# One written order for all five engines of an attention-and-Fourier kernel, with the MLP weights in four transfers

## The chip, the cores and the metric

The kernel runs on one core of one Trainium2 chip. A core has five engines that this kernel uses: TensorE (PE, matrix products, with a weight load that the profile lists as PEld), VectorE (DVE), ScalarE (ACT), GpSimd (POOL) and SyncE (SP, which here only issues transfers). The metric is the device time of one execution in microseconds, smaller is better; the figure of a kernel is the median of its runs.

## The reference, cut to what matters

Two stages follow each other. The first is block-sparse causal attention for 4 batches, 8 heads, 768 positions and head size 64: every query keeps its own block of 64 keys and the three blocks with the highest gate score. The second takes the heads side by side as a 768 x 512 matrix per batch, adds the real part of its two-dimensional Fourier transform, normalizes each row, and runs a two-layer MLP (512 to 2048 to 512) with a residual.

```python
k_rep = k.reshape(B, H, n_blocks, block, D).mean(axis=3)
gate_scores = np.einsum('bhsd,bhnd->bhsn', q, k_rep)      # causal blocks only
top_idx = np.argsort(gate_scores, axis=-1)[..., -top_k:]
scores = scale * np.matmul(q, k.transpose(0, 1, 3, 2))    # masked to those blocks, causal
attn = np.exp(scores - max); attn = attn / sum
x = np.matmul(attn, v)                                    # -> (B, 768, 512)
# ...
u = x + np.real(fft(fft(x, axis=1), axis=2))
un = (u - mean(u)) / np.sqrt(var(u) + 1e-06)
out = u + np.maximum(un @ w_ch1, 0.0) @ w_ch2
```

## The kernel before: the parts that the change touches

Heads are worked on in pairs, so there are 16 pairs P = 0 to 15, four to a batch. The steps of a pair and of a batch have short names, which the texts below use:

| name | what it does | engine |
|---|---|---|
| Lk, Lq, Lv | loads k, q, v of a pair | SyncE |
| tk, tq | six 128x128 transposes of k or q | PE |
| ks, kc, qc, qs | sums of k by block, copies of k and q | DVE, ACT, DVE, GpSimd |
| g, gt, gx, gm, K | gate scores, transpose, top three, mask, mask into the k/q rows | PE, DVE, DVE, DVE, GpSimd |
| s, e, d | one of six score tiles, its exponential, its causal edge | PE, ACT, GpSimd |
| vc, v, x | copy of v to 16 bits, product with v, division by the sums | GpSimd, PE, DVE |
| fs, fd, f (fa, fb) | folds of x over rows and columns, before the Fourier products | DVE |
| y, ty, tr, m, u, xu, xt, un | Fourier products, copies, second product, u, centred x, its transpose | PE, ACT, DVE, PE, DVE, ACT, PE, DVE |
| w, r | one of 16 tiles of the first MLP layer, its ReLU | PE, ACT or DVE |
| c, o | second MLP layer for 128 rows, residual | PE, DVE |

Attention for the first seven pairs and 12 of batch 0's MLP tiles stand in one written list, `HEAD`, in whose order all five engines work. What comes after is woven from two lists by weights, with only SyncE's order fixed; the other four engines' order is left to the scheduler of the tile framework.

```python
HEAD = """
Lkq:2 Lv:0 Lv:1 tk:0 tq:0 Lkq:3 tk:1 ks:0 qc:0 ks:1 g:0 gt:0 tq:1 Lkq:4 gx:0 tk:2 gm:0 qc:1 qs:0
# ... 16 lines cut
gm:5 d:4,2 kc:6 v:3 d:4,4 e:4,3 x:3 qs:6 s:5,2 s:4,5 s:5,5 e:5,2 fs:3 s:5,0 e:4,5 s:5,4 s:5,1 Lw:2
d:4,5 e:5,5 s:5,3 fd:3 e:5,0 g:6 fb:0 e:5,1 fa:0 d:5,5 e:5,4 Lw:3 d:5,2 gt:6 gx:6 vc:4 Lv:6 gm:6
d:4,3 y:1 y:0 d:4,1 v:4 d:5,0 ty:1 e:5,3 s:6,3 d:5,4 tr:1 ty:0 d:5,1 e:6,3 m:0 tr:0 s:6,4 x:4
# ... 6 lines cut
"""
# ...
    def fold_s(b, hp):                       # two DVE instructions in a row
        # ...
        tt(sd[:, 0, :, cols], x_b[:, 0:3, cols], x_b[:, 3:6, cols], ALU.add)
        tt(sd[:, 1, :, cols], x_b[:, 0:3, cols], x_b[:, 3:6, cols], ALU.subtract)
    # ...
    def fg_hi(b):                            # fg_lo is alike, for the other half
        fg, zw = fg_tile(b)
        tt(fg[:, :, 257:384], zw[:, :, 257:384], zw[:, :, 511:384:-1], ALU.subtract)
        tt(fg[:, :, 384:511], zw[:, :, 257:384], zw[:, :, 511:384:-1], ALU.add)
        nc.vector.tensor_copy(out=fg[:, :, 511:512], in_=zw[:, :, 384:385])
    # ...
    def load_w1(dt):                         # 4 of these, 128 rows x 2048 columns each
        nc.gpsimd.dma_start(out=w1_sb[:, dt, :], in_=moe_w_ch1[128 * dt:128 * (dt + 1), :])

    def load_w2(c):                          # 4 of these, 512 rows each
        nc.gpsimd.dma_start(out=w2_sb[:, 4 * c:4 * (c + 1), :],
                            in_=moe_w_ch2[512 * c:512 * (c + 1), :]
                            .rearrange("(it p) l -> p it l", p=128))
    # ...
    with tc.manual_schedule(engines={ET.SP, ET.PE, ET.DVE, ET.Activation, ET.Pool}):
        consts_first()
        for x in HEAD.split():
            n, a = x.split(":")
            HEAD_OPS[n](*[int(i) for i in a.split(",")])
    with tc.manual_schedule(engines={ET.SP}):
        for b in range(B):
            L = []
            for i in range(NP * (b + 1) + 1, min(NP * (b + 2) + 1, NPAIR + 1)):
                if i > 7:
                    L += attn_slot(i, i + 1, i + 2)
            weave(L, stream(b) if b else stream_0())
```

`tt` is `tensor_tensor` on DVE unless another engine is named. GpSimd's copies (`pcopy`, used by qs, K and vc) and the causal edges d are `affine_select` instructions with one input in the on-chip memory SBUF. The transfers that GpSimd issues turn the weights from 32 to 16 bits on the way.

Of the kernel before, what the change touches and what calls it, by code (L numbers as in the profile page):

```python
# [124 lines left out]
NW = 12  # L125


HEAD = """
Lkq:2 Lv:0 Lv:1 tk:0 tq:0 Lkq:3 tk:1 ks:0 qc:0 ks:1 g:0 gt:0 tq:1 Lkq:4 gx:0 tk:2 gm:0 qc:1 qs:0
kc:0 kc:1 s:0,2 kc:2 vc:0 Lv:2 qs:1 e:0,2 s:0,4 g:1 tq:2 Lkq:5 e:0,4 ks:2 d:0,2 gt:1 gx:1 s:0,5  # L130
qc:2 e:0,5 s:0,0 e:0,0 s:0,3 s:0,1 gm:1 g:2 s:1,2 e:0,1 s:1,3 gt:2 e:0,3 d:0,0 e:1,2 s:1,4 d:0,4
tk:3 gx:2 d:0,1 e:1,3 d:0,5 d:0,3 e:1,4 v:0 gm:2 qs:2 ks:3 x:0 s:1,0 kc:3 tq:3 Lkq:6 Lt:0 e:1,0
vc:1 Lv:3 s:2,0 s:1,1 s:1,5 qc:3 d:1,0 e:2,0 g:3 s:2,2 d:1,3 d:1,4 fs:0 e:1,5 gt:3 s:2,1 d:1,5
d:2,0 s:2,5 gx:3 e:1,1 tk:4 e:2,2 e:2,5 gm:3 d:1,2 d:1,1 s:2,3 e:2,1 tq:4 Lkq:7 v:1 ks:4 qs:3 qc:4
e:2,3 g:4 kc:4 d:2,1 x:1 gt:4 fs:1 s:2,4 gx:4 d:2,5 s:3,0 d:2,2 tk:5 e:2,4 s:3,2 qs:4 ks:5 e:3,0
vc:2 Lv:4 s:3,4 e:3,2 d:2,3 d:2,4 kc:5 v:2 s:3,3 Lc:0 gm:4 x:2 tq:5 Lkq:8 qc:5 fs:2 vc:3 Lv:5
e:3,4 s:3,5 s:4,1 e:3,3 s:3,1 s:4,0 fd:2 e:3,5 g:5 e:4,1 d:3,0 Lw:0 d:3,3 gt:5 gx:5 s:4,4 e:4,0
tq:6 e:3,1 qc:6 d:3,2 d:3,4 d:3,5 Lw:1 d:3,1 tk:6 Lkq:9 qs:5 e:4,4 s:4,2 d:4,0 e:4,2 ks:6 s:4,3
gm:5 d:4,2 kc:6 v:3 d:4,4 e:4,3 x:3 qs:6 s:5,2 s:4,5 s:5,5 e:5,2 fs:3 s:5,0 e:4,5 s:5,4 s:5,1 Lw:2
d:4,5 e:5,5 s:5,3 fd:3 e:5,0 g:6 fb:0 e:5,1 fa:0 d:5,5 e:5,4 Lw:3 d:5,2 gt:6 gx:6 vc:4 Lv:6 gm:6  # L140
d:4,3 y:1 y:0 d:4,1 v:4 d:5,0 ty:1 e:5,3 s:6,3 d:5,4 tr:1 ty:0 d:5,1 e:6,3 m:0 tr:0 s:6,4 x:4
s:6,0 e:6,4 u:0 m:1 u:1 d:5,3 e:6,0 m:2 u:2 xu:0 s:6,1 s:6,5 tq:7 qc:7 e:6,5 vc:5 Lv:7 xu:1 xt:0
tk:7 Lkq:10 e:6,1 un:0 ks:7 xt:1 d:6,5 xu:2 v:5 xt:2 un:1 un:2 kc:7 g:7 qs:7 s:6,2 Li:0 gt:7 w:10
gx:7 w:4 e:6,2 tk:8 x:5 r:10 r:4 w:11 gm:7 tq:8 Lkq:11 Lx:0 K:7 vc:6 Lv:8 kc:8 qc:8 w:0 d:6,0 ks:8
w:9 Lx:1 d:6,4 g:8 r:11 r:0 s:7,2 s:7,3 r:9 s:7,4 gt:8 d:6,1 d:6,3 d:6,2 gx:8 e:7,2 tq:9 e:7,4
qc:9 v:6 qs:8 e:7,3 fs:5 s:7,5 e:7,5 s:7,1 s:7,0 x:6 w:7 w:1 e:7,1 r:7 Lx:2 qs:9 w:5 e:7,0 r:5
fs:4 w:6 tk:9 Lkq:12 w:3 gm:8 fs:6 r:6 d:7,3 fd:6 ks:9 r:1 r:3 d:7,2 Lx:3 K:8 w:8 kc:9 w:2 d:7,5
r:8 d:7,0 r:2 d:7,1 d:7,4
# [5 lines left out]
def kernel(  # L154
# [58 lines left out]
    w1_sb = ctile([128, NDT, DF], F16, "w1_sb")  # L213
# [8 lines left out]
    dummy = ctile([128, 1], FP, "dummy")  # L222
    wsrc = bpool.tile([128, 512], F16, tag="hT0", name="zeros")
# [6 lines left out]
    hold = [None]  # L230

    def load(P, who, eng):
        if hold[0] is not None:
            hold[0].append((P, who, eng))
            return
        b, hp = divmod(P, NP)
        src = (q, k, v)[who]
        if who == 2:
            t = apool.tile([128, 2 * NST, 64], FP, tag="nat2", name=f"nat2_{P}", bufs=2)
            eng.dma_start(t, src[b, 2 * hp:2 * hp + 2].rearrange("e (st p) d -> p (e st) d", p=128))  # L240
            nat[P, 2] = t
            return
        if P >= NPAIR:
            return
        t = apool.tile([128, NST, 2, 64], FP, tag=f"nat{who}", name=f"nat{who}_{P}", bufs=3)
        for e in range(2):
            eng.dma_start(t[:, :, e, :],
                          src[b, 2 * hp + e].rearrange("(st p) d -> p st d", p=128))
        nat[P, who] = t
# [4 lines left out]

    def cast_v(P):
        v_cast(P)
        if P + 2 < NPAIR:
            load(P + 2, 2, nc.sync)
# [12 lines left out]
    def a_sums(P):  # L271
        ps = pairs[P]["tp", 1]
        kr12 = spool.tile([128, NB], FP, tag="kr12", name=f"kr12_{P}")
        nc.vector.tensor_reduce(out=kr12, in_=ps.rearrange("p (n c) -> p n c", c=64),  # L274
                                axis=mybir.AxisListType.X, op=ALU.add)
        tt((kr_s if P < NX else kr2_s)[P % NSLOT][:, :, 0:NB],
# [22 lines left out]

    def stage_A(P):  # L300
        a_tp(P, 1)
        a_sums(P)
        a_k(P)
        a_tp(P, 0)
        a_q32(P)
        a_q(P)
# [36 lines left out]
    def g_mask(P):  # L343
        d = pairs[P]
        mx = d["mx"]
        if P < NX:
            gt, l = d["gt"].rearrange("p (b n) -> p b n", n=32), lt[:, :, 0:NB]
            tt(l, gt[:, :, 0:NB], mx[:, :, 2:3].to_broadcast([128, 10, NB]), ALU.is_lt)
            tt(l, l, oth, ALU.mult)
            full = lt.rearrange("p b n -> p (b n)")  # L350
        else:
            full = apool.tile([128, 192], F16, tag="ltb", name=f"lt_{P}", bufs=1)
            tt(full.rearrange("p (j n) -> p j n", n=16),
               d["gt"].rearrange("p (j n) -> p j n", n=16),
               mx[:, :, 2:3].to_broadcast([128, 12, 16]), ALU.is_lt)
            tt(full, full, oth2, ALU.mult)
        mt = apool.tile([128, 320 if P < NX else 192], F16, tag="mt", name=f"mt_{P}", bufs=4)
        nc.vector.transpose(out=mt, in_=full)  # L358
        d["mt"] = mt

    def stage_G(P):
        g_mm(P)
        g_turn(P)
        g_max(P)
        g_mask(P)
# [48 lines left out]
    def stage_S(P, i):  # L414
        s_mm(P, i)
        s_exp(P, i)
        s_sel(P, i)

# [24 lines left out]
    def stage_V(P, e):  # L443
        v_mm(P, e)
        if e == 1:
            v_x(P)

# [3 lines left out]
    def fold_s(b, hp):  # L451
# [6 lines left out]
        tt(sd[:, 0, :, cols], x_b[:, 0:3, cols], x_b[:, 3:6, cols], ALU.add)  # L458
        tt(sd[:, 1, :, cols], x_b[:, 0:3, cols], x_b[:, 3:6, cols], ALU.subtract)

    def fold_d(b, hp):
        sd, zw = fold[b]
        cols = slice(128 * hp, 128 * hp + 128)
        if hp >= 2:
            sf = sd.rearrange("p a t d -> p (a t) d")
            lo = slice(128 * (hp - 2), 128 * (hp - 1))
            tt(zw[:, :, lo], sf[:, :, lo], sf[:, :, cols], ALU.add)
            tt(zw[:, :, cols], sf[:, :, lo], sf[:, :, cols], ALU.subtract)

    def stage_fold(b, hp):  # L470
        fold_s(b, hp)
        fold_d(b, hp)
# [8 lines left out]
    def fg_lo(b):  # L481
        fg, zw = fg_tile(b)
        tt(fg[:, :, 1:128], zw[:, :, 1:128], zw[:, :, 255:128:-1], ALU.add)
        nc.vector.tensor_copy(out=fg[:, :, 0:512:256], in_=zw[:, :, 0:512:256])
        nc.vector.memset(fg[:, :, 128:129], 0.0)
        tt(fg[:, :, 129:256], zw[:, :, 1:128], zw[:, :, 255:128:-1], ALU.subtract)

    def fg_hi(b):
        fg, zw = fg_tile(b)
        tt(fg[:, :, 257:384], zw[:, :, 257:384], zw[:, :, 511:384:-1], ALU.subtract)  # L490
        tt(fg[:, :, 384:511], zw[:, :, 257:384], zw[:, :, 511:384:-1], ALU.add)
        nc.vector.tensor_copy(out=fg[:, :, 511:512], in_=zw[:, :, 384:385])

    def stage_fg(b):
        fg_lo(b)
        fg_hi(b)

    ys, y_ps, m_ps, t_ps = {}, {}, {}, {}
# [33 lines left out]

    def stage_Y(b, h):
        y_mm(b, h)
        y_copy(b, h)
        y_turn(b, h)
# [39 lines left out]
    def stage_M(b, kp):  # L576
        m_mm(b, kp)
        m_u(b, kp)
        m_x(b, kp)
        if b not in (0, B - 1):  # L580
            stage_T(b, kp)

# [7 lines left out]
    def t_copy(b, kp):  # L590
        ps, dst = t_ps[b, kp], un_t[b][:, :, 256 * kp:256 * kp + 256]
        if b == 0 or kp < 2:
            nc.vector.tensor_copy(out=dst, in_=ps)
        else:
            nc.vector.tensor_copy(out=dst[:, :, 0:128], in_=ps[:, :, 0:128])
            nc.scalar.copy(out=dst[:, :, 128:256], in_=ps[:, :, 128:256])

    def stage_T(b, kp):
        x_b = x_t[b]
        if b in (0, B - 1):  # L600
            t_mm(b, kp)
            t_copy(b, kp)
            return
        for kt in range(2 * kp, 2 * kp + 2):
            nc.sync.dma_start_transpose(un_t[b][:, :, 128 * kt:128 * kt + 128], x_b[:, kt, :])

    def stage_R(b):

        mv, rs, _ = st_t[b]
        for kt in range(NST):  # L610
            bst = spool.tile([128, 6], FP, tag="bst", name=f"bst{kt}_{b}", bufs=4)
            nc.vector.bn_stats(out=bst, in_=u_t[b, kt // 2][:, kt % 2, :])
            nc.vector.bn_aggr(out=mv[:, kt, :], in_=bst)
        vr, t2 = [spool.tile([128, NST], FP, tag=n, name=f"{n}_{b}") for n in ("vr", "t2")]
        yi = rs.bitcast(I32)
        po = nc.gpsimd
# [5 lines left out]
                                op0=ALU.mult, op1=ALU.add)  # L622
        for _ in range(3):
# [6 lines left out]
    def w1_mm(b, it):  # L630
        unT = un_t[b]
        h_t[b, it, "p"] = hp = pst([128, S], f"h{it}_{b}")
        for dt in range(NDT):
            w1s = w1_sb[:, dt, 128 * it:128 * (it + 1)]
# [14 lines left out]
    def stage_W1(b, it):  # L649
        w1_mm(b, it)  # L650
        w1_relu(b, it)

    def stage_W2(b, sts, part):
        n = len(sts)
        if part == 0:
            h_t[b, "c"] = pst([128, n, 512], f"c{sts[0]}_{b}")
        cps = h_t[b, "c"]
        st = sts[part]
        for it in range(NIT):
            nc.tensor.matmul(cps[:, part, :], h_t[b, it][:, 128 * st:128 * (st + 1)],  # L660
# [153 lines left out]
    def run(L):  # L814
        for f, _ in L:
            f()
# [63 lines left out]
```

## Time and profile before

| | |
|---|---|
| time, median of 3 runs | 321.04 us (320.4 to 322.42) |
| span of the profiled execution | 321.2 us |
| mean granted TensorE clock | 0.983 |
| busy: DVE, ACT, POOL | 200.6 us, 166.7 us, 109.4 us |
| first transpose on PE, first instruction of W2 (`L660`) | 6.3 us, 107.7 us |
| last product of W2 ends, span ends | 317.4 us, 321.2 us |
| SyncE's loads and stores; GpSimd's weight transfers | 27.69 MB, 38.7% of 16 transfer engines; 4.19 MB as written, 8.0% |

In the profile's lines of groups, a line begins with the line of the kernel (L12), the engine and the operation; `fg<-zw` means that tile fg is written from tile zw; shapes are partitions x elements. Durations there are in nanoseconds, all other times in microseconds. A digit in the strip of 40 slices is the busy share of that slice (8 us each) in tenths. The granted clock is given as a share of full speed.

### The profile page before, as it was taken

Reading aid. Unit: us, or ns where it says so; the run is one execution under the profiler, and the core shown is the slowest. Engines: PE = TensorE matmul, PEld = TensorE weight load, DVE = VectorE, ACT = ScalarE, POOL = GpSimd, SP = SyncE. Lnnn points to the kernel's source line nnn. Section 1 sums busy time; section 2 is a strip of 40 time slices with the busy share of each in tenths; the row PEclk is TensorE's granted clock in tenths of the full one; section 3 lists DMA queues with packets and bytes.
Section 4 is the critical chain, followed back from the end, with each engine's and each line's share of the span. In section 5 each row is a group of like instructions: output and inputs, shape, how many; then the busy total and the mean of one; then the engine's idle time right before and its main releaser. Section 6 shows DMA issues by size and latency. Waiting matters only on the chain.

```text
span 321.2 us, 6693 instructions
## 1 busy us (share of the span) xinstructions
PE 298.7 (93%) x2638; PEld 180.4 (56%) x2638; DVE 200.6 (62%) x577; ACT 166.7 (52%) x206; POOL 109.4 (34%) x247
## 2 busy tenths in 40 slices
PE   8788976969998999989999999999999999999995
PEld 3456654656654545645666646645665565565442
DVE  2899999797794358975545549984314379421211
ACT  1688973775728444655767443637573124344000
POOL 2166295144894223346452524234220000200000
PEclk9999997999997999999999999999999999999999
DMA  9999999989993421169600012144000101100023
GB/s 175 217 214 217 259 198 220 228 168 168 202 155 70 98 74 43 35 139 253 152 0 2 0 56 61 35 131 117 0 2 0 43 24 68 65 2 0 0 82 116
DMA packets 88843, 32.83 MB, mean 102 GB/s; under 512 B 82592, under 2 KB 84972, under 8 KB 88812
## 3 DMA queue, kind: packets, MB, share of 16 engines
q1 hardware_dynamic: 83932, 27.69, 38.7%
q0 software_dynamic: 2688, 4.19, 8.0%
q10 hardware_dynamic: 2192, 0.52, 0.9%
q8 instruction: 21, 0.34, 0.4%
q14 instruction: 10, 0.08, 0.1%
HBM read 28.73 MB, written 6.29 MB: 109 GB/s over the span
## 4 chain that ended last, share of the span: by engine, by line
PE 66%; DVE 22%; ACT 7%; DMA 2%; issue 1%; SPq 1%; POOL 0%; DVEq 0%
PE c L660 22%; PE h L635 16%; PE h L637 8%; PE sc L390 6%; PE tp L269 4%; PE av L428 3%; ACT pt L405 3%; DVE sd L192 2%; DVE fg L192 2%; PE yp L508 2%; DVE kr L274 2%; DVE zw L192 2%; DMA nat<-in_k_dram 2%; DVE u L666 2%; DVE u L561 2%; DVE lt L192 1%
## 5 line engine op out<-in xcount | busy, mean ns | idle before, releaser
L405 ACT ACTIVATE pt<-sc 128x1024 f16<-128x1024 f32 (+1 forms) x96 | 84.0, 922 | 48.6 <-PE sc L390 41.6
L660 PE MATMUL c<-w_sb,hT 128*128 128x512 f16 x384 | 87.3, 379 | 0.0
L635 PE MATMUL h<-unT,w_sb 128*128 128x512 f16 x256 | 86.4, 383 | 0.6 <-ACT pt L405 0.6
L637 PE MATMUL h<-unT,w_sb 128*128 128x256 f16 x256 | 70.3, 275 | 0.0
L411 POOL TENSOR_SCALAR_AFFINE_SELECT pt<-pt 128x256 f16<-128x256 f16 x96 | 39.4, 426 | 82.2 <-ACT pt L405 81.7
L660 PEld LDWEIGHTS <-hT 128*128 128x128 f16 x384 | 36.8, 98 | 41.0 <-issue 0.5
L647 ACT ACTIVATE hT<-h 128x768 f16<-128x768 f32 x48 | 38.7, 810 | 31.1 <-PE h L637 30.8
L666 DVE SCALAR_TENSOR_TENSOR u<-c,rs,u 128x512 f32<-128x512 f32 x24 | 17.1, 742 | 40.1 <-PE c L660 40.1
L635 PEld LDWEIGHTS <-w_sb 128*128 128x128 f16 x256 | 25.1, 98 | 28.7 <-issue 1.7
L645 DVE TENSOR_SCALAR hT<-h 128x768 f16<-128x768 f32 x16 | 15.3, 955 | 34.6 <-PE h L637 34.5
L390 PE MATMUL sc<-qk 96*128 96x512 f16 (+3 forms) x144 | 27.8, 308 | 4.1 <-DVE hT L645 1.8
L269 PE MATMUL tp<-id,nat 128*128 128x128 f32 x192 | 26.1, 276 | 5.2 <-DMA nat<-in_k_dram 1.4
L637 PEld LDWEIGHTS <-w_sb 128*128 128x128 f16 x256 | 25.2, 98 | 4.9 <-issue 0.8
L195 POOL TENSOR_SCALAR_AFFINE_SELECT qk<-q 64x768 f16<-64x768 f32 (+1 forms) x25 | 20.6, 826 | 19.6 <-DVE q L290 18.9
L428 PEld LDWEIGHTS <-pt 128*128 128x128 f16 x672 | 23.7, 97 | 5.6 <-POOL pt L411 1.8
L269 PEld LDWEIGHTS tp<-id,nat 128*128 128x128 f32 x192 | 21.2, 141 | 10.0 <-issue 1.7
L428 PE MATMUL av<-v,pt 128*128 128x65 f16 x672 | 25.1, 193 | 1.2 <-POOL pt L411 1.2
L195 POOL TENSOR_SCALAR_AFFINE_SELECT v<-nat 128x768 f16<-128x768 f32 x16 | 14.8, 931 | 23.5 <-DMA nat<-in_v_dram 23.2
L195 POOL TENSOR_SCALAR_AFFINE_SELECT qk<-mt 32x384 f16<-32x384 f16 x36 | 18.7, 521 | 7.8 <-DVE mt L358 6.0
L573 ACT ACTIVATE x<-u,nm 128x512 f16<-128x512 f32 x24 | 15.8, 713 | 9.4 <-DVE nm L567 9.4
L390 PEld LDWEIGHTS <-qk 96*128 96x128 f16 x144 | 12.5, 99 | 13.8 <-issue 3.1
L285 ACT CAST qk<-tp 64x768 f16<-64x768 f32 x18 | 14.3, 793 | 10.4 <-DVE kr L274 10.3
(84 smaller groups left out, 352.8 us busy)
## 6 DMA issues: line engine op xcount, KB each, us to landing
nat<-in_v_dram SPq DMA_DIRECT2D x16, 384.0 KB, 5.7
nat<-in_k_dram SPq DMA_DIRECT2D x31, 192.0 KB, 5.3
nat<-in_q_dram SPq DMA_DIRECT2D x31, 192.0 KB, 4.0
out_dram<-u SPq DMA_DIRECT2D x11, 512.0 KB, 2.9
w_sb<-in_moe_w_ch_dram POOLq DMA_DIRECT2D x8, 512.0 KB, 7.9
fs_sb<-c_FS SPq DMA_DIRECT2D x1, 582.0 KB, 5.0
out_dram<-u SPq DMA_DIRECT2D x2, 256.0 KB, 2.0
fd_sb<-c_FD SPq DMA_DIRECT2D x1, 384.0 KB
```

The lines of the kernel that those rows point to most:

```text
L192: (eng or nc.vector).tensor_tensor(out=out, in0=in0, in1=in1, op=op)
L195: nc.gpsimd.affine_select(out=out, in_=in_, pattern=[[0, i] for i in n], base=0, channel_multiplier=0, compare_op=ALU.is_ge, fill=0.0)
L269: nc.tensor.transpose(ps[:, 128 * st:128 * st + 128], src[:, st, :], id32)
L390: nc.tensor.matmul(ps[:, e, co:co + q1 - q0], qk[0:96, e, 1, 128 * jt:128 * jt + 128], qk[0:96, e, 0, q0:q1], start=True, stop=True)
L405: nc.scalar.activation(out=d["pt"][:, o:o + 2 * n].rearrange("p (e c) -> p e c", e=2), in_=d["sc", i][:, :, 0:n], func=AF.Exp, scale=0.125)
L411: nc.gpsimd.affine_select(out=dg, in_=dg, pattern=[[0, 2], [1, 128]], base=0, channel_multiplier=-1, compare_op=ALU.is_ge, fill=0.0)
L428: nc.tensor.matmul(av[:, e, 66 * st:66 * st + 65], pt[:, co:co + 128], vv[:, e, jt, 0:65], start=(cnt == 0), stop=(cnt == 20))
L635: nc.tensor.matmul(hp[:, 0:512], w1s, unT[:, dt, 0:512], start=(dt == 0), stop=(dt == NDT - 1))
L637: nc.tensor.matmul(hp[:, 512:768], w1s, unT[:, dt, 512:768], start=(dt == 0), stop=(dt == NDT - 1))
L647: nc.scalar.activation(out=hT, in_=hp, func=AF.Relu)
L660: nc.tensor.matmul(cps[:, part, :], h_t[b, it][:, 128 * st:128 * (st + 1)], w2_sb[:, it, :], start=(it == 0), stop=(it == NIT - 1))
L666: nc.vector.scalar_tensor_tensor(out=o[:, i, :], in0=cps[:, i, :], scalar=st_t[b][1][:, sts[i]:sts[i] + 1], in1=o[:, i, :], op0=ALU.mult, ...
```

## The change

The written list now covers the whole kernel and is called `ORDER`; weaving, weights and held-back loads are gone, and all five engines follow the list to the end. Several steps are split so that the list can place their parts apart: `ks` becomes ks and kh, the mask becomes gl (two parts) and gm, each fold becomes two or four single instructions (fs, fd, f with a part number), the row statistics become bn for each 128 rows, nv and nr, a second-layer product becomes two halves of eight products (c:b,st,h), and each 128 rows of the output have their own residual (o) and store (od). Loads of k and q are placed one by one.

`pg` is new: GpSimd copies four elements, one from each of the four folded pieces f, so that it waits until all four are there. `w1_sb` becomes two tiles by column halves, and the weights come in four transfers (W:0, W:1, X:0, X:1) instead of eight.

The purpose is to have one order that is laid out as a whole, with GpSimd held back while DVE makes the folded pieces, and with the transfers of the weights put between GpSimd's copies.

```diff
-HEAD = """
-Lkq:2 Lv:0 Lv:1 tk:0 tq:0 Lkq:3 tk:1 ks:0 qc:0 ks:1 g:0 gt:0 tq:1 Lkq:4 gx:0 tk:2 gm:0 qc:1 qs:0
 (cut)
+ORDER = """
+Lq:1 Lk:1 Lq:2 Lk:2 tk:0 tq:0 ks:0 Lq:3 Lk:3 qc:0 tq:1 iz:1 kh:0 qs:0 g:0 Lq:4 Lv:0 Lv:1 qc:1 iz:0
 (cut)
+fd:3,1 s:4,2 gt:6 e:5,2 s:5,4 f:0,3 s:5,3 e:4,2 f:0,2 tk:8 f:0,1 e:5,4 y:0,1 f:0,0 e:5,3 ks:8
+d:5,4 d:4,2 y:0,0 tr:0,1 d:5,3 kc:8 W:0 gx:6 d:4,1 s:4,5 d:5,1 ty:0,1 tr:0,0 tk:7 d:5,0 pg:0 d:4,3
+e:4,5 ks:7 ty:0,0 m:0,2 W:1 gl:6,0 kc:7 d:5,2 m:0,1 u:0,2 d:5,5 vc:5 m:0,0 u:0,1 xu:0,2 d:4,4 Lv:7
+Lk:10 v:5 qs:6 u:0,0 qs:7 xu:0,1 xt:0,2 tq:8 xu:0,0 un:0,2 d:4,5 xt:0,1 kh:8 qc:8 xt:0,0 kh:7
+gl:6,1 v:4 qs:8 un:0,1 un:0,0 gm:6 g:7 vc:6 x:5 w:0,1 Lv:8 Lq:11 gt:7 x:4 w:0,3 r:0,1 gx:7 s:6,5
 (cut)
+e:10,5 K:11 Lv:14 Lq:15 xu:1,1 x:8 s:10,2 c:0,0,0 e:10,2 un:1,1 fs:8,1 d:10,4 fs:8,0 s:10,3 d:10,2
 (cut)
+c:3,1,1 o:3,4 od:3,4 c:3,5,1 o:3,1 od:3,1 o:3,0 od:3,0 o:3,5 od:3,5
 """
-    w1_sb = ctile([128, NDT, DF], F16, "w1_sb")
+    w1_s = [ctile([128, NDT, DF // 2], F16, f"w1_{c}") for c in range(2)]
+    gone = ctile([1, 4], F16, "gone")
 (cut)
-    def fg_hi(b):
-        fg, zw = fg_tile(b)
-        tt(fg[:, :, 257:384], zw[:, :, 257:384], zw[:, :, 511:384:-1], ALU.subtract)
-        tt(fg[:, :, 384:511], zw[:, :, 257:384], zw[:, :, 511:384:-1], ALU.add)
-        nc.vector.tensor_copy(out=fg[:, :, 511:512], in_=zw[:, :, 384:385])
+    def fg(b, i):
 (cut: i == 0 and i == 1)
+        elif i == 2:
+            tt(fg[:, :, 257:384], zw[:, :, 257:384], zw[:, :, 511:384:-1], ALU.subtract)
+            nc.vector.tensor_copy(out=fg[:, :, 256:257], in_=zw[:, :, 256:257])
+        else:
+            tt(fg[:, :, 384:511], zw[:, :, 257:384], zw[:, :, 511:384:-1], ALU.add)
+            nc.vector.tensor_copy(out=fg[:, :, 511:512], in_=zw[:, :, 384:385])
+
+    def fg_wait(b):
+        nc.gpsimd.tensor_copy(out=gone, in_=fg_tile(b)[0][0:1, 0, 127:512:128])
 (cut)
-    def load_w1(dt):
-        nc.gpsimd.dma_start(out=w1_sb[:, dt, :], in_=moe_w_ch1[128 * dt:128 * (dt + 1), :])
+    def load_w1(c):
+        h = slice(DF // 2 * c, DF // 2 * (c + 1))
+        nc.gpsimd.dma_start(out=w1_s[c],
+                            in_=moe_w_ch1[:, h].rearrange("(dt p) l -> p dt l", p=128))
     def load_w2(c):
-        nc.gpsimd.dma_start(out=w2_sb[:, 4 * c:4 * (c + 1), :],
-                            in_=moe_w_ch2[512 * c:512 * (c + 1), :]
+        nc.gpsimd.dma_start(out=w2_sb[:, 8 * c:8 * (c + 1), :],
+                            in_=moe_w_ch2[1024 * c:1024 * (c + 1), :]
                             .rearrange("(it p) l -> p it l", p=128))
 (cut)
-    with tc.manual_schedule(engines={ET.SP}):
-        for b in range(B):
-            L = []
-            for i in range(NP * (b + 1) + 1, min(NP * (b + 2) + 1, NPAIR + 1)):
-                if i > 7:
-                    L += attn_slot(i, i + 1, i + 2)
-            weave(L, stream(b) if b else stream_0())
+        for x in ORDER.split():
+            n, a = x.split(":")
+            WORK[n](*[int(i) for i in a.split(",")])
```

## The prediction

> **What bounds the kernel now.** I read the page first: the span, the busy shares and the strip of slices.
>
> ```profile
> span 321.2 us, 6693 instructions
> PE 298.7 (93%) x2638; PEld 180.4 (56%) x2638; DVE 200.6 (62%) x577; ACT 166.7 (52%) x206; POOL 109.4 (34%) x247
> ...
> PE   8788976969998999989999999999999999999995
> ...
> DVE  2899999797794358975545549984314379421211
> ...
> PEclk9999997999997999999999999999999999999999
> DMA  9999999989993421169600012144000101100023
> ```
>
> TensorE is busy 93% of the span, so a new order can win little more than its 22.5 us of idle time, its slow-clock time and the gaps inside "busy". All of that lies to the left: there PE's digits are 6 to 9, DVE's mostly 7 to 9, the transfer engines' 8 or 9. From slice 18 on PE is full. The windows put numbers on it (the columns are the stretch, its length, then PE, weight loads, DVE, ACT and POOL busy with counts, the granted clock, the transfer share and GB/s):
>
> ```profile
> 0.00:100.00 100.00, 85.88 (x1008) 56.32 (x1009) 84.27 (x253) 66.67 (x83) 52.60 (x117) 0.96 1.05 200
> 100.00:140.00 40.00, 37.38 (x305) 22.25 (x304) 27.26 (x82) 21.60 (x28) 13.68 (x25) 0.98 0.27 60
> 140.00:322.00 182.00, 175.47 (x1329) 101.87 (x1327) 89.10 (x245) 78.43 (x97) 43.08 (x105) 1.00 0.21 57
> ```
>
> PE idles 14.1 us in the first 100 us (and until the first transpose at 6.3 us it runs only warm-up products), 2.6 in the next 40, and 6.5 in the rest, of which 3.8 are the tail (the last product ends at 317.4). DVE is at 84% in the first stretch. What it does there is partly waiting inside instructions; the timeline of DVE, GpSimd and PE around the first fold:
>
> ```profile
> 49.12 4.20 DVE L192 TENSOR_TENSOR fg<-zw 128x762 f16<-128x762 f16 x2
> ...
> 49.30 0.55 POOL L728 DMA_DIRECT2D w_sb<-in_moe_w_ch_dram  x1
> 49.86 0.42 POOL L411 TENSOR_SCALAR_AFFINE_SELECT pt<-pt 128x256 f16<-128x256 f16 x1
> 50.22 0.91 POOL L195 TENSOR_SCALAR_AFFINE_SELECT v<-nat 128x768 f16<-128x768 f32 x1
> 51.07 1.83 POOL L411 TENSOR_SCALAR_AFFINE_SELECT pt<-pt 128x256 f16<-128x256 f16 x5
> ...
> 54.02 3.25 PE L508 MATMUL yp<-fs_sb,fg 128*128 128x193 f16 x19 [2.69 <-DVE fg L484]
> ```
>
> Two fg instructions take 4.20 us together; they end when GpSimd's unbroken row of work ends (52.9), and PE, which waited 2.69 us for fg, then makes 19 products in 3.25 us. The group of fg shows that this is no normal duration:
>
> ```profile
> L192 DVE TENSOR_TENSOR fg<-zw x16: 545/554/3635, 49.1 to 259.6; 128x762 f16<-128x762 f16 x16
> ```
>
> Median 554 ns, longest 3635 ns.
>
> **What the Trainium skill says.** "SBUF — State Buffer", section "Who interferes with whom": a DVE instruction with two SBUF inputs and a GpSimd instruction that reads SBUF contend for one port, and the one that comes second blocks for the other's whole duration. The trace agrees (554 against 3635 ns). "TensorE: Matmul & The Clock Gate", Part 1: an idle window of about 3.4 us halves the TensorE clock, and a busy one restores it. The trace agrees in kind: granted clock 0.83 between 40 and 60 us, around that wait, and yp products of 368 ns against a least of 243. "DMA: Bandwidth & Descriptors", section "Queues, rings and completion order": each transfer engine takes turns between the queues that have work. So GpSimd's weights and SyncE's loads should slow each other; here a weight transfer of 512 KB as written landed 7.2 to 8.7 us after issue, against 25.7/8 = 3.2 us of engine time (8.0% of the span over eight transfers).
>
> **The change, part by part.** The products stay the same. I price each step by its measured group: tk/tq 0.66 us, g 0.74 (early) or 0.46, a large score tile about 0.45, v 1.29, y 1.0 (1.5 with the extra row), m 0.87, a W1 tile w 1.30, half a W2 row block c 1.73. Over all steps PE comes to 277 us. As a test: the last 42.0 us of dense work (275.4 to 317.4) are priced at 16 x 1.30 + 12 x 1.73 = 41.6, so I add 1%: 280.
>
> *Contention, head.* Removed: the excess of the two-input DVE forms. fg is 16 x 752 ns mean against 545 least, 3.3 us; sd 32 x (484 - 345), 4.4 us; zw 16 x (634 - 546), 1.4 us; the copy in fg 0.7 us; masks and key sums some 3 us. Sum about 13 us of DVE time, nearly all before 100 us. `pg` is not in front of the folds but behind them; it is the placing that helps: in the list no GpSimd copy stands between f:0,3 and f:0,0, and d:5,4, GpSimd's next, waits for an exponential of that moment. I count 8 of the 13 us as gone. PE gains only what it waited for: the 2.7 us at the fold, and about 2 us of half clock after it.
>
> *Split steps.* Adds 4 small copies on DVE (about 0.18 us each) and, for the last batch, one whole copy on DVE in place of a half each on DVE and ACT: under 1 us, beside PE work.
>
> *Head as a whole.* I sum each engine's work in the list up to marks. Up to the first W2 half (c:0,0,0) DVE has 107.5 us: key sums and q copies 26.9, gate 28.2, x 9 x 1.18 = 10.6, folds 16.1, tr, u, un, bn, ReLU and the rest 25.5. PE has 92.8 there (W1 20.8, scores 23.8, transposes 17.1, v 12.9, g 7.5, y, m, xt 10.7). DVE starts its sums at 7.15 us, so if the list is laid out in time, as I read it, the first c cannot start before 7.15 + 107.5 = 114.7. It is *later* than now (107.7), with much more PE work in front. Now DVE idles 13.5 us between 7.15 and 107.7 (87.1 busy of 100.6: the first window's 84.3 less 0.9 before 7.15, and 3.7 after 100), and contention is extra. For the new list I allow 5 us for idle time and remaining contention together: first c at 119.5.
>
> *Rest.* Behind that mark PE has c 83.0, W1 62.4, scores 13.1, v 7.7, m 6.1, y 5.0, transposes 4.0, g 1.8, xt 1.3: 184.5, with 1% 186.4. DVE has 102 there, ACT 81, GpSimd 46, so PE bounds it. Stalls: 1.5 us, near the 1.9 us that PE idles between 140 and 317.4 now. The last residual (0.74 us) and store keep the tail at 3.8 us; the last store was already 256 KB.
>
> Sum: 119.5 + 186.4 + 1.5 + 3.8 = 311.2. I predict 311.
>
> **Rivals.** *The transfers become the bound.* A pair's k, q or v is 393 KB; at the 216 GB/s of the early slices that is 1.82 us, and all 48 take 87; the weights 25.7, tables and constants 5: 118 us. Summed in the list's order from 2.5 us on, the tables have landed at 49.0 where DVE's sum reaches their first use (y:0,1) at 49.3; W:0 at 64.5 against its use at 65.3; v of pair 3 at 38.9 against 38.8. There is no slack: the list is cut to the transfers as closely as to DVE. For: share 1.05 in the first 100 us; W:0 is twice as long as each old one and issued later, just after the first y, and shares turns with loads. Against: before landed all four quarters of W1 between 41.4 and 58. If transfers run 5% slower, the head slips 3 to 6 us: 314 to 317.
>
> *A fixed order stalls where the scheduler's did not.* An engine that meets an unready step stops though later ones are ready. For: the old written head is where PE idles; the stretch 140 to 240, woven, has PE at 98.75 of 100 us. Against: that head suffered from contention, and behind 120 us the list keeps W1 and W2 work between the attention steps. If each of the three later batch changes costs 3 us: 320, no gain.
>
> *Contention gone altogether and DVE full.* First c at 116, then no stall: 116 + 186.4 + 3.8 = 306. For: the marks of DVE, transfers and use agree within a microsecond, so the list was made with good durations. Against: nothing in the list keeps fs and fd clear of GpSimd.
>
> **Range and chances.** The 306 and the 317 are equally near; 305 to 318 holds both. Faster by over 2% means below 314.6, that is 3.6 us above my sum, well inside the first rival. I give it 0.72, within 2% 0.23, slower 0.05, since a loss of 6 us would need stalls where PE is now full.
>
> **What would show it.** Right: fg's longest duration under 1.5 us and the first y at 50 to 52 us (now 54.0); first W1 at 66 to 69 (now 73.1); first c at 117 to 122; DVE above 90% up to there; PE idle below 3 us between 140 us and the end of W2. The loads are the bound if PE or GpSimd wait longest for nat or w1 tiles. Wrong: PE idle of several us behind 120, or first c beyond 124.

## The result, and the profile after

| | before | after |
|---|---|---|
| time, median | 321.73 us (320.4 to 324.4, 4 runs) | 306.88 us (306.41 to 307.28, 4 runs) |
| span of the profiled execution | 321.2 us | 305.2 us |
| mean granted TensorE clock | 0.983 | 1.000 |
| PE idle in the span | 22.5 us | 13.4 us |
| first y, first w, first c | 54.0, 73.1, 107.7 us | 52.0, 66.0, 115.0 us |

The changed kernel takes 0.9528 of the time (95% interval 0.9461 to 0.9594): 14.9 us less. The page of the changed kernel:

```profile
span 305.2 us, 6705 instructions
...
PE 291.8 (96%) x2638; PEld 179.2 (59%) x2638; DVE 194.4 (64%) x581; ACT 163.2 (53%) x205; POOL 106.5 (35%) x247
...
PE   7789996999999999999999999999999999999994
...
PEclk9999999999999999999999999999999999999999
DMA  9999989999999998610110001112200011100013
```

PE makes the same 2638 products in 6.9 us less busy time; the clock strip, which had two slices below 9, has none. The transfers are now full to slice 16 (before: to slice 11): they were spread out over a longer head. The windows, in the columns used for the kernel before:

```profile
0.00:100.00 100.00, 90.91 (x1117) 61.37 (x1118) 85.17 (x290) 73.95 (x92) 52.91 (x111) 1.00 1.08 205
100.00:140.00 40.00, 39.87 (x387) 25.80 (x386) 34.28 (x106) 29.58 (x38) 27.08 (x59) 1.00 0.70 140
140.00:306.00 166.00, 161.04 (x1137) 92.08 (x1134) 74.95 (x188) 59.70 (x77) 26.48 (x78) 1.00 0.12 41
```

PE idles 9.1 us in the first 100 us instead of 14.1, 0.1 in the next 40 instead of 2.6. A third of the gain is not idle time at all: three stretches at half clock, shown below, took 5.1 us of PE's work in the kernel before, and now there are none. (A clock of 0.983 over 321.2 us makes 5.5 us; the rest of it lies behind the last product and costs nothing.) 9.1 us less idle time and 5.1 us of clock make 14.2 of the 16.0 us by which the span is shorter; the other 1.8 us are shorter busy time at full clock. The timeline of DVE, GpSimd and PE around the first fold of the changed kernel:

```profile
48.75 0.51 DVE L239 TENSOR_TENSOR fg<-zw 128x762 f16<-128x762 f16 x1
49.26 0.55 DVE L239 TENSOR_TENSOR fg<-zw 128x762 f16<-128x762 f16 x1
49.80 1.02 DVE L239 TENSOR_TENSOR fg<-zw 128x762 f16<-128x762 f16 x2
...
50.49 1.30 POOL L442 TENSOR_SCALAR_AFFINE_SELECT pt<-pt 128x256 f16<-128x256 f16 x3 [2.98 <-ACT pt L436]
51.74 0.96 POOL L713 DMA_DIRECT2D w<-in_moe_w_ch_dram  x1
...
52.01 1.78 PE L523 MATMUL yp<-fs_sb,fg 128*128 128x193 f16 x19 [2.04 <-DVE kr L311]
```

The four fg instructions take their 0.5 us each; GpSimd stood idle for 2.98 us just then. PE still waits 2.04 us, but the 19 products behind take 1.78 us, not 3.25. The wait is put down to DVE's kr, but when the same kernel was run again the products started at 50.7 us while kr ended at 51.8, so they do not need kr. They also wait for the Fourier table, whose load was issued only at 45.70, and in four of the later runs the wait in this place is named as the table's (`DMA fs_sb<-c_FS`; 0.6 us in three of them, 3.0 in the one with W1 earlier).

Where did the clock go? Windows of 2 us of the kernel before (length, PE busy, granted clock, transfer share, GB/s):

```profile
44.00:46.00 2.00, 1.23 (x26) 1.00 1.03 184
46.00:48.00 2.00, 1.32 (x20) 0.79 0.96 157
48.00:50.00 2.00, 2.00 (x24) 0.50 1.04 208
50.00:52.00 2.00, 1.34 (x20) 0.86 1.10 242
52.00:54.00 2.00, 0.00 (x0) 0.99 1.08 216
54.00:56.00 2.00, 1.98 (x13) 0.50 1.09 217
56.00:58.00 2.00, 2.00 (x15) 0.66 1.03 220
...
96.00:98.00 2.00, 0.43 (x2) 1.00 1.27 255
98.00:100.00 2.00, 2.00 (x17) 0.58 0.44 77
100.00:102.00 2.00, 2.00 (x10) 0.56 0.00 0
102.00:104.00 2.00, 2.00 (x17) 1.00 0.00 0
```

There are three stretches at half clock, each behind a thin stretch of PE. Their length follows from the columns: 54 to 58 us is 2 x (2.00 x 0.50 + 2.00 x 0.34) = 3.4 us, and the other two give 3.4 as well. Each takes 1.7 us of PE's work on top of the gap.

This is one execution, and not every execution of the kernel before has three such stretches. Over the 53 that ran beside the last group of experiments the mean clock lies between 0.983 and 0.995, 0.987 on average, which is a loss of 4 us and not of 5.5. The same 53 show what a stretch costs: the 20 at 0.983 or 0.984 have a median of 324.2 us, the 24 at 0.987 to 0.989 one of 322.6, the nine at 0.992 to 0.995 one of 321.0, so 1.6 us for each step. The eight executions of the changed kernel here and in the next section have 0.997 to 1.000.

### The profile page after: what moved, and what is told of

It is laid out like the page before. It is cut to its first block, busy times and chain, and to the rows that moved or that the text cites. A ratio compares the mean times of both kernels' runs of the same rounds, so it can differ in the third digit from the quotient of the medians.

```text
span 305.2 us, 6705 instructions
## 1 busy us (share of the span) xinstructions
PE 291.8 (96%) x2638; PEld 179.2 (59%) x2638; DVE 194.4 (64%) x581; ACT 163.2 (53%) x205; POOL 106.5 (35%) x247
## 4 chain that ended last, share of the span: by engine, by line
PE 80%; DVE 12%; DMA 4%; ACT 2%; SPq 1%; issue 1%; DVEq 0%
PE c L652 27%; PE h L633 18%; PE h L635 9%; PE sc L421 6%; PE av L454 5%; PE tp L306 4%; DMA nat<-in_q_dram 4%; PE yp L523 3%; DVE u L571 2%; PE sc L416 2%; ACT pt L436 1%; PE g L357 1%; PE sc L427 1%; PE mx L557 1%; PE mx L558 1%; DVE tr L543 1%
## 5 line engine op out<-in xcount | busy, mean ns | idle before, releaser
L652 PE MATMUL c<-w_sb,hT 128*128 128x512 f16 x384 | 86.0, 379 | 0.0
L633 PE MATMUL h<-unT,w 128*128 128x512 f16 x256 | 84.7, 379 | 0.0
L635 PE MATMUL h<-unT,w 128*128 128x256 f16 x256 | 69.7, 272 | 0.0
L633 PEld LDWEIGHTS <-w 128*128 128x128 f16 x256 | 25.0, 98 | 28.9 <-issue 0.4
L635 PEld LDWEIGHTS <-w 128*128 128x128 f16 x256 | 25.0, 98 | 3.5
L421 PE MATMUL sc<-qk 96*128 96x512 f16 (+3 forms) x144 | 26.6, 305 | 0.1
L239 POOL TENSOR_TENSOR t<-vr,rs 128x6 f32<-128x6 f32 x12 | 2.5, 207 | 60.5 <-DVE rs L614 59.8
L454 PEld LDWEIGHTS <-pt 128*128 128x128 f16 x672 | 22.1, 97 | 2.3 <-issue 1.0
L454 PE MATMUL av<-v,pt 128*128 128x65 f16 x672 | 23.0, 193 | 0.2
L571 DVE SCALAR_TENSOR_TENSOR u<-mx,x 128x512 f32<-128x512 f32 x24 | 15.5, 684 | 8.7 <-DMA out_dram<-u 4.4
L537 ACT CAST ty<-yp 128x772 f16<-128x772 f32 x8 | 8.0, 1045 | 19.2 <-PE yp L523 18.0
## 6 DMA issues: line engine op xcount, KB each, us to landing
w_sb<-in_moe_w_ch_dram POOLq DMA_DIRECT2D x2, 1024.0 KB, 14.1
```

Source lines behind the costliest of these rows:

```text
L421: nc.tensor.matmul(ps[:, e, co:co + q1 - q0], qk[0:96, e, 1, 128 * jt:128 * jt + 128], qk[0:96, e, 0, q0:q1], start=True, stop=True)
L454: nc.tensor.matmul(av[:, e, 66 * st:66 * st + 65], pt[:, co:co + 128], vv[:, e, jt, 0:65], start=(cnt == 0), stop=(cnt == 20))
L571: nc.vector.scalar_tensor_tensor(out=u_b[:, k2, :].rearrange("p (m two) -> p two m", two=2), in0=mps[:, k2, :].rearrange("p (two m) -> p t ...
L633: nc.tensor.matmul(hp[:, 0:512], w1s, unT[:, dt, 0:512], start=(dt == 0), stop=(dt == NDT - 1))
L635: nc.tensor.matmul(hp[:, 512:768], w1s, unT[:, dt, 512:768], start=(dt == 0), stop=(dt == NDT - 1))
L652: nc.tensor.matmul(c_ps[b, g[0]][:, st - g[0], :], h_t[b, it][:, 128 * st:128 * (st + 1)], w2_sb[:, it, :], start=(it == 0), stop=(it == N ...
```

## The experiments

Every time is a median, beside runs of the kernel before on the same chip. The changed kernel, run again with the first group, is the measure for its variants; where a variant ran on another chip, the ratio to before is the better measure than the microseconds. Three of the questions: is it DVE against GpSimd at the fold (theory A), the written order behind the first c (C) or only the head (D), and what do the weights' transfers do (E)?

### The changed kernel once more

> The changed kernel once more, to have its time beside the next three on the same chip. Expected: 306.9 us, within 0.5; first product with the folded pieces (y) at 52.0 us, longest fg near 1.05 us, clock 1.00.

306.33 us, ratio to before 0.9513 (0.9447 to 0.9579); y at 50.7, first c at 114.0 us, clock 0.997, longest fg 1046 ns. y moves by 1.3 us between two executions of the same kernel.

### GpSimd set opposite the fold again: copies, and memsets

```diff
+    scr = ctile([128, 640], F16, "scr")
+    def pz(_):
+        for _i in range(5):
+            pcopy(scr, czr, [S - Q0])          # a_copy5
+            # nc.gpsimd.memset(scr, 0.0)       # a_set5 instead
-e:5,2 s:5,4 f:0,3
+e:5,2 s:5,4 pz:0 f:0,3
```

> The changed kernel with five needless GpSimd copies (128x640, 16 bits, SBUF to SBUF) set opposite the folds of batch 0. Theory A (the old head lost time because DVE's two-input folds wait while GpSimd reads SBUF, and the gap on PE then halves its clock for some 3.4 us): the copies run from about 47.5 to 51 us, the longest fg is above 2 us, y starts at 53.5 to 54.5 instead of 52.0, the mean clock falls below 0.995, total 309 to 311. Theory B (GpSimd beside DVE is harmless, the gain is from the placing of the steps alone): fg stays below 1.1 us, total within 1 us of 306.9.

> The same with five memsets of the same tile in place of the five copies: GpSimd is as busy in the same place, but reads nothing. Theory A, as a matter of reading SBUF: fg stays below 1.1 us, y at 52.0, total within 0.7 us of 306.9. If it is only that GpSimd gets late with its own work (the causal edges behind), or if writing contends as well: like the copies, 309 to 311.

The copies: 308.45 us (0.9571, 0.9517 to 0.9626), 2.1 us more. The memsets: 306.66 us (0.9522), the same as without. The timeline of DVE and GpSimd with the copies,

```profile
46.62 1.34 DVE L239 TENSOR_TENSOR sd<-x 128x384 f16<-128x384 f16 x2
47.89 3.04 DVE L239 TENSOR_TENSOR zw<-sd 128x768 f16<-128x768 f16 x3
...
46.92 4.58 POOL L242 TENSOR_SCALAR_AFFINE_SELECT scr<-czr 128x640 f16<-128x640 f16 x5
```

and with the memsets:

```profile
49.51 0.55 DVE L239 TENSOR_TENSOR fg<-zw 128x762 f16<-128x762 f16 x1
...
50.05 1.02 DVE L239 TENSOR_TENSOR fg<-zw 128x762 f16<-128x762 f16 x2
...
47.72 3.38 POOL L513 MEMSET scr<- 128x640 f16 x5
```

The two sets did not stand opposite the same steps, so each is compared with the same step beside nothing. The copies (46.9 to 51.5 us) met two sd and three zw: the zw take 1.06 us each, where one alone takes 0.55, and the two sd 1.34 us together, where an undisturbed one takes 0.35. The memsets (47.7 to 51.1 us) met the last zw and all four fg, and these take 0.52 to 0.55 us each, as they do without memsets. I had expected fg to be hit by the copies (its longest stays at 1046 ns): they began earlier than I meant and struck the fold's steps before it. All the same fg begins at 51.3 instead of 48.6. PE then waits twice, and the windows show the clock fall:

```profile
50.00:52.00 2.00, 0.59 (x5) 1.00 1.04 336
52.00:54.00 2.00, 1.26 (x11) 0.81 1.33 240
54.00:56.00 2.00, 2.00 (x14) 0.50 1.35 214
56.00:58.00 2.00, 2.00 (x18) 0.84 1.15 194
```

The 19 y products take 3.10 us. So theory A holds in its narrow form: GpSimd work that reads SBUF slows DVE's two-input instructions, work that only writes does not. That is what the Trainium skill states on the page "SBUF — State Buffer", section "Who interferes with whom".

### Without pg

```diff
-ty:0,1 tr:0,0 tk:7 d:5,0 pg:0 d:4,3        # and pg:1 to pg:3
+ty:0,1 tr:0,0 tk:7 d:5,0 d:4,3
```

> The changed kernel without pg, the four-element copies that make GpSimd wait for the folded pieces. Theory A as I read the trace: in batch 0 pg stands behind the folds and waits for nothing (it runs at 53.8 us, the fold ends at 51.1), in later batches PE has other work; total within 0.6 us of 306.9, fg's longest at most 1.6 us. Rival (pg is what keeps GpSimd off): fg's longest above 2 us in some batch and total 309 or more.

306.17 us (0.9517, 0.9454 to 0.958), clock 1.000, longest fg 1047 ns. In this order the explicit hold does nothing that the placing of the steps doesn't do already.

### The order behind the first c left to the scheduler

```diff
-        for x in ORDER.split():
+        todo = ORDER.split()
+        cut = todo.index("c:0,0,0")
+        for x in todo[:cut]:
             n, a = x.split(":")
             WORK[n](*[int(i) for i in a.split(",")])
+    with tc.manual_schedule(engines={ET.SP}):
+        for x in todo[cut:]:
+            n, a = x.split(":")
+            WORK[n](*[int(i) for i in a.split(",")])
```

> The changed kernel with the written order only up to the first product of W2 (c:0,0,0); behind it the same list is given out, but only SyncE keeps to it and the scheduler of the tile framework orders the other four engines, as in the kernel before. Theory C (a good half of the gain lies in the order behind the head: before, PE had gaps of 0.3 to 1.8 us at the batch changes between 107 and 140 us): first c unchanged at 115.0, PE idle 2 to 4 us between there and the last product, total 308.5 to 311. Theory D (the gain is all in the head, before the first c; any order that keeps MLP work at hand fills PE afterwards): PE idle there under 0.7 us, total within 1 us of 306.3.

310.93 us (0.9631, 0.9584 to 0.9677): 4.6 us more by the medians, 3.8 by the ratios (0.0118 of 321.7). The place shows in the window and in PE's timeline:

```profile
110.00:120.00 10.00, 7.55 (x107) 5.70 (x106) 7.84 (x31) 6.11 (x9) 8.66 (x24) 0.83 0.47 96
```

```profile
115.56 2.49 PE L454 MATMUL av<-v,pt 128*128 128x65 f16 x42 [2.45 <-POOL pt L442]
```

PE waits 2.45 us for a causal edge. GpSimd's timeline says why it came late:

```profile
110.01 0.20 POOL L239 TENSOR_TENSOR t<-vr,rs 128x6 f32<-128x6 f32 x1
...
113.12 0.24 POOL L239 TENSOR_TENSOR rs<-rs,t 128x6 f32<-128x6 f32 x1
113.32 1.71 POOL L242 TENSOR_SCALAR_AFFINE_SELECT qk<-q 64x768 f16<-64x768 f32 x2
115.09 1.49 POOL L442 TENSOR_SCALAR_AFFINE_SELECT pt<-pt 128x256 f16<-128x256 f16 x4
```

From 110.0 to 115.0 GpSimd does the twelve little instructions of the row statistics (nr) and two copies of q, and only then the four edges that finish the tenth pt. In the written order these four stand ahead of both; so the scheduler had put steps from behind the cut before steps from ahead of it. Gap and half clock (1 - 0.83 of 10 us) make 4.2 us, and the first c is at 118.7 instead of the 115.0 that I had expected to stay. From 140 us on PE has no idle time in either kernel. So C has the size right but not the place, and D is right about all that follows the hand-over.

This loss is one that the variant itself makes, at its own hand-over; it is not the one that the kernel before has. There PE never runs at half clock behind the first c, and idles 4.45 us up to its last product, nearly all of it in ten gaps of 0.2 to 0.75 us between 117 and 259 us; in the changed kernel it idles 0.08 us there (length, PE busy, clock, transfers):

```profile
107.70:317.30 209.60, 205.15 (x1585) 1.00 0.22 57
```

```profile
115.00:301.05 186.05, 185.97 (x1335) 1.00 0.17 47
```

So the order behind the first c is worth about 4.4 us by these two lines. That a_sched loses nearly as much is chance. It also shows that the scheduler, given the new list and the split steps, leaves none of those ten gaps, so leaving the order to it is not by itself what makes them.

### Eight transfers by rows, and W1's transfers earlier

```diff
-    w1_s = [ctile([128, NDT, DF // 2], F16, f"w1_{c}") for c in range(2)]
+    w1_s = [ctile([128, NDT // 2, DF], F16, f"w1_{c}") for c in range(2)]    # a_8rows
 (cut: two transfers of 128 rows at each place of W, two of 512 rows at each of X)
```

```diff
-Lv:5 ks:6 s:4,0 vc:4 e:4,4 v:3 gm:5 Lv:6 Lq:9 Lk:9 Lq:10 e:4,0              # a_wearly
+Lv:5 ks:6 s:4,0 vc:4 e:4,4 v:3 gm:5 Lv:6 W:0 Lq:9 Lk:9 Lq:10 e:4,0
-kc:6 d:4,0 s:5,1
+kc:6 d:4,0 W:1 s:5,1
 (cut: W:0 and W:1 taken out behind kc:8 and m:0,2)
```

> The changed kernel with the weights in eight transfers again, W1 cut by rows (two row blocks at the place of W:0, two at W:1), everything else as it is. Each W1 tile then needs both places' transfers. If the column halves are worth what they look like: the first W1 product waits for the second pair, which lands at about 66 to 68 us, so it starts up to 2 us later than 66.0, and total is 306.8 to 308.5; GpSimd gives some 1.2 us more to issuing. If the number and the cut of the transfers do not matter: within 0.6 us of 306.3.

> The changed kernel with the two transfers of W1 some 10 us earlier, at about 41 and 45 us, where the kernel before had its first. If the loads bound the head (transfer share 1.08 there): 4.2 MB of weights go ahead of the tables and of k, q and v of the next pairs, y starts at 55 to 58 instead of 51 to 52, PE falls to half clock, total 309 to 313. If DVE bounds it and transfers have slack: y at 51 to 52, total within 1 us of 306.3.

By rows: 307.14 us (0.9508, 0.9467 to 0.9549). The first W1 product waits 1.5 us for weights, as it should; the total can't be told from the changed kernel's. The number and the cut of the transfers are worth 0.8 us by the medians, and with an interval of 1.3 us to each side that may be nothing.

Earlier: 314.38 us (0.973, 0.9683 to 0.9777), 7 us more by the ratios, for an issue at 46.4 and 47.8 us instead of 51.7 and 54.3. PE's waits in that kernel:

```profile
PE av L454 <- POOL v L242: 3.4, 1, 3.4
PE yp L523 <- DMA fs_sb<-c_FS: 3.0, 1, 3.0
```

The tables come 3.0 us late, and y starts at 53.5 us (expected: 55 to 58). Then a v comes late, GpSimd's copy of it as well (it waits up to 10.9 us for that transfer), and PE's product 3.35 us. Behind both PE runs at half clock: 42 av products take 2.47 us, priced at 1.29. Every later mark slips alike (first c at 123.0 against 114.0). There is no slack in the transfers between 45 and 70 us.

### The tables earlier

```diff
-Lv:4 Lk:7 Lk:8 LT:0 kh:5
+Lv:4 LT:0 Lk:7 Lk:8 kh:5
 (cut: tk:8, ks:8 and kc:8 moved behind y:0,0)
```

> The changed kernel with the Fourier tables loaded two loads of k earlier, and the transposes of k of pair 8 behind the first Fourier products instead of before them, so that those products need 393 KB less before them. In the trace of the changed kernel they wait 2.04 us; I take the tables for the cause (their load is issued at 45.7 and the wait ends at 52.0), not the DVE reduction that the profile names. If so, y starts at 49.8 to 50.5 and total is 304.5 to 306. If the wait was for DVE, y stays at 51 to 52 and total within 0.6 us of 306.3; if the bytes are only moved, a later wait takes it back, and total is within 0.6 us as well, with y earlier.

307.93 us (306.78 to 309.03; 0.9521, 0.9468 to 0.9574). y starts at 49.9 as expected, and nothing comes of it: PE now waits 1.6 us for k and 1.7 us for tr, and the first w is at 67.1, not 65.1 to 66.0. The bytes were only moved.

### The kernel before, with one cause taken away

```diff
-e:4,1 d:3,0 Lw:0 d:3,3                     # b_wlate: all four Lw leave their places ...
+e:4,1 d:3,0 d:3,3
-d:4,3 y:1 y:0 d:4,1 v:4 d:5,0 ty:1 e:5,3 s:6,3 d:5,4 tr:1
+d:4,3 y:1 y:0 Lw:0 d:4,1 v:4 Lw:1 d:5,0 ty:1 e:5,3 s:6,3 Lw:2 d:5,4 Lw:3 tr:1
```

```diff
-e:5,1 fa:0 d:5,5                           # b_pg; b_both has both edits
+e:5,1 fa:0 pg:0 d:5,5
```

> The kernel before with one thing changed: its four transfers of W1 issued behind the first Fourier products (about 52 to 59 us) instead of between 41 and 49 us. Theory E (in the head transfers are short, so weights that go ahead of k, q and v cost time; moving W1 5 us earlier in the changed kernel cost 8 us): the loads of pairs 5 to 8 land earlier, total 316 to 319, that is 3 to 6 less than before. Rival (the kernel before loses its head time to DVE and GpSimd, and the weights are hidden there): within 1.5 us of before; or slower, if the first W1 product at 73 us then waits for weights.

> The kernel before with one thing changed: GpSimd holds still (a copy of four elements of the folded pieces stands in front of its next causal edge) until batch 0's fold is done. Theory A: the longest fg falls from 3635 ns to below 1.5 us, y starts at 50.5 to 52 instead of 54.0, and no or less half clock follows; total 2.5 to 5 us less than before. Rival (the fold is not on the path, or GpSimd's own work is late then and gives it back): within 1.5 us of before.

> The kernel before with both: W1 issued later and GpSimd held during the fold. If the two causes are separate their gains add: 312 to 316 us. If the weights' issue was itself what GpSimd and DVE clashed over, or both only shorten the same wait for the fold: no better than the better of the two alone.

| | median us | ratio to before | 95% interval | y at, us | longest fg, ns |
|---|---|---|---|---|---|
| b_wlate | 318.40 | 0.9871 | 0.9809 to 0.9934 | 51.9 | 755 |
| b_pg | 319.29 | 0.9895 | 0.9869 to 0.9921 | 51.2 | 561 |
| b_both | 319.78 | 0.9885 | 0.9857 to 0.9913 | 51.0 | 561 |

Each alone gains 3.4 to 4.2 us by its ratio, as expected, and they do not add. (Five of b_both's 18 executions were over 1.5% slower than its fastest, the profiled one among them, and its ratio leaves them out; the other 13 have a median of 318.70 us.) The group of fg in b_wlate, and the timeline of its fold, say why at least in part:

```profile
L192 DVE TENSOR_TENSOR fg<-zw x16: 543/552/755, 49.0 to 253.1; 128x762 f16<-128x762 f16 x16
```

```profile
47.77 2.09 POOL L411 TENSOR_SCALAR_AFFINE_SELECT pt<-pt 128x256 f16<-128x256 f16 x3 [1.72 <-ACT pt L405]
...
48.96 1.32 DVE L192 TENSOR_TENSOR fg<-zw 128x762 f16<-128x762 f16 x2
...
49.82 1.22 POOL L195 TENSOR_SCALAR_AFFINE_SELECT v<-nat 128x768 f16<-128x768 f32 x1
```

Moving the weights alone brings fg from 3635 to 755 ns. GpSimd's edges and its copy of v still stand opposite the fold, but Lw:3, which GpSimd issued from 49.30 to 49.85 in the kernel before, is gone from that row. So both edits end the same long wait, b_pg by moving GpSimd's row and b_wlate by taking the issue out of it, and the gains do not add. Theory E, that the loads then land earlier, is not borne out: PE waits for no load of q, k or v between 30 and 108 us in either trace, and GpSimd's waits for v there are 8.5 us before and 8.9 in b_wlate. The total that E named (316 to 319) came, but not by E's path.

In b_pg the long wait has only moved. GpSimd issues Lw:3 later, and the next two-input step of DVE pays (for lt the least is 0.28 us):

```profile
52.19 0.55 POOL L732 DMA_DIRECT2D w_sb<-in_moe_w_ch_dram  x1
...
52.92 3.01 DVE L192 TENSOR_TENSOR lt<-gt,mx 128x120 f16<-128x120 f32 x1
...
53.96 2.23 POOL L412 TENSOR_SCALAR_AFFINE_SELECT pt<-pt 128x256 f16<-128x256 f16 x6
```

In the fourteen traces of this case nine DVE steps lose more than 1 us, all in the kernel before and its variants, and each of them began 0.4 to 1.0 us after GpSimd began to issue a weight transfer; no other step loses more than 0.8 us. Not every step behind an issue is hit, and why these are is not shown. What b_pg gains is for the most part clock: over its 20 executions the mean clock is 0.996, against 0.987, which is 2.9 of the 3.4 us.

### Needless products in the gap

```diff
+        if b == 0 and h == 1:
+            for _ in range(44):
+                nc.tensor.matmul(yps[:, 0, 400:512], wsrc[:, 0:128], wsrc[:, 0:112], start=True, stop=True)
```

> The kernel before with 44 needless products of zeros (112 columns) on PE just before the first Fourier products, in the time in which PE waits for the fold (51.3 to 54.0 us): the wait stays, PE is not idle in it. If the half clock at 54.0 to 57.3 us follows from that idle time: y still starts at 54.0, the clock is 1.00 between 54 and 57.5, the 19 products take about 1.8 us instead of 3.25, and the total falls by 1 to 2 us. If the clock does not depend on it: no change in clock, total within 0.7 us of before.

322.11 us (0.9973, 0.9944 to 1.0003): the gain, some 0.9 us, can't be told from none. But the mechanism is there; PE's timeline and windows, in a run in which this stage was 1.4 us later:

```profile
52.67 2.34 PE L505 MATMUL yp<-zeros 128*128 128x112 f16 x44
55.37 1.79 PE L511 MATMUL yp<-fs_sb,fg 128*128 128x193 f16 x19 [0.36 <-DVE fg L484]
```

```profile
50.00:52.00 2.00, 2.00 (x22) 0.50 1.13 253
52.00:54.00 2.00, 2.00 (x39) 0.97 1.11 225
54.00:56.00 2.00, 1.64 (x29) 1.00 1.05 209
56.00:58.00 2.00, 2.00 (x23) 1.00 0.88 183
```

fg is as late as ever (3635 ns), PE is not idle, and the second half-clock stretch is gone: 19 products in 1.79 us. The first one, behind the thin stretch before, is still there. The third, at 98 us, is gone in this execution too, though nothing was done to it, so one trace alone would not prove the point. The executions do: the mean clock of the 20 is 0.994 against 0.987, about one stretch less (0.0065 of 320 us is 2.1 us). So the half clock follows PE's idle time, not what caused it. Why less than half of the 2.1 us comes back as time stays open.

## Why the prediction was right, and where it was off

I said 311 us, 305 to 318; it is 306.88. The marks: first y at 50 to 52 us, it is 52.0; first w at 66 to 69, it is 66.0; longest fg below 1.5 us, it is 1.05; DVE above 90% up to the first c, it is 91% (98.2 of 107.9 us); PE idle below 3 us behind 140 us up to the last product, it is 0.1 us from 116.5 to 301.0. One mark was missed: first c at 117 to 122, it is 115.0.

*Right in mechanism and size: the rest.* From the first c to the last product I had 186.4 us; it took 186 (115.0 to 301.1). Pricing PE's steps by their dense rates and adding 1% was enough for a stage in which PE has no idle time. The allowance of 1.5 us for stalls there was not needed. The tail is 4.2 us, for 3.8.

*Off in size: "I allow 5 us for idle time and remaining contention together: first c at 119.5".* It is 115.0, and that the sum in front of the allowance gave 114.7 is luck: two errors cancel. DVE's steps up to there were priced at 107.5 us, but DVE was busy for 98.2 between 7.15 and 115.0; I had priced them by mean durations, and consecutive records overlap (over all steps my prices make 209.5 us, while DVE was busy for 200.6 in the kernel that I priced and for 194.4 in the changed one). And DVE was not busy for 9.6 us there, nearly twice the 5 us allowed. Whether DVE or the transfers bound the head is not separated.

*Off in size: "about 2 us of half clock after it".* I counted one stretch at the first fold; the profiled execution had three, 5.1 us in all, and the changed kernel has none. That term was in the profile before: one minus the clock of 0.983, times the span.

*Half right: "the 2.7 us at the fold".* In the profiled execution PE still waits 2.04 us there, most likely for the tables; run again, 0.6 us, for fg. What went for certain is the half clock behind it.

*Read too smoothly: "The trace agrees (554 against 3635 ns)".* It agrees that the two engines collide, not on how long one instruction blocks the other. The longest GpSimd instruction beside that fg takes 0.91 us, and fg lost 3.1 us to a whole row of them. Where GpSimd's copies stood alone beside the fold (a_copy5) a step lost 0.5 us.

*A term left out.* My sum was in the span's time, and the time of an execution is about 2 us more than its span (307.28 for 305.2; before 322.88 for 321.2). It hid part of the error: span 305.2 against 311.2, 4.5 us of it in front of the first c and 1.5 us of stalls behind it that did not come.

*Contention, 8 of 13 us gone.* By the same groups: fg 752 to 579 ns, sd 484 to 364, zw 634 to 608, 7.0 us over their 64 instructions; DVE's busy time fell by 6.2. That it is the placing and not pg was right: without pg, 306.17. The placing did one thing that I had not seen: no fold stands behind an issue of weights any more (they are at 51.7, 54.3, 85.6 and 86.5 us).

*The rivals.* The transfers are the bound of the head in the sense that their sum has no slack: W1 issued 5.3 and 6.5 us earlier costs 7 us, tables earlier gain nothing. They did not slip, so the cost of 3 to 6 us did not come. The rival that a fixed order would stall where the scheduler's did not was wrong in sign: behind the first c PE idles 4.45 us in the woven kernel and 0.08 in the fixed order.

*Where the time lies.* By the two profiles, 16.0 us of span: 5.0 us less PE idle time up to the first c (14.1 to 9.1), 4.4 us less from there to the last product, 5.1 us of half clock in the head, 1.8 us of other busy time, and 0.3 us given back in the tail. Of the head's share b_pg and b_wlate each win 3.4 to 4.2 us in the kernel before, at the fold and by the half clock. The rest of the head, in which PE also gains at 90 to 108 us (1.8 us idle and 1.6 us of clock in the kernel before), was not taken apart, nor were the split steps and the loads placed one by one. The cut of the weights is not among the causes; their place is a condition for all of it.

## What to carry to other kernels

A gap on PE can cost twice, once as idle time and once as 3.4 us at half clock behind it; look for the two together, and count the clock's loss (one minus the mean clock, times the span, over several executions) as part of what a better order may win. When an order is written by hand, place GpSimd's work that reads SBUF away from DVE's two-input steps (here 0.55 us became 1.06), above all the row that follows GpSimd's issue of a transfer (here up to 3.6 us); five memsets beside the folds cost nothing that could be measured. Sum the transfers against their first uses: where they met within a microsecond here, weights that went ahead of what was needed next cost 7 us.

## What was not expected

- A gap of well under 3.4 us is enough for a half-clock stretch: waits of 1.64 and 0.74 us within 3.2 us in a_copy5, 2.45 us in a_sched. Yet a wait of 2.04 us in the changed kernel brought none (clock 1.000).
- The clock changes on a beat. In the kernel before it halves at 47.1, 54.0 and 98.3 us, for 3.41 us each; the distances are 2 and 13 times that length, and in all fourteen traces the time between two changes is a whole multiple of it. So it matters where on the beat a gap falls. PE was busy for 52, 23 and 47% of the beat before each of those three, and for 46% of the one that holds the changed kernel's wait (50.2 to 53.6 us), behind which the clock stayed full: no threshold comes out of these figures.
- Five GpSimd copies of 0.9 us each cost 2.1 us of total time; five memsets of 0.7 us at the same place in the list 0.3, which is within the spread.
- The two transfers of W1, 1024 KB each as written, landed 9.5 to 12.8 us after issue beside SyncE's loads; issued some 6 us earlier, 12.2 to 16.6.
